# Attention and a two-layer MLP in one kernel: pools that wait tile by tile, a reordered end of attention, and the x of the next visit one unit earlier

## The chip, the cores and the metric

The kernel runs on one core of a Trainium2 chip. It drives five engines: PE (TensorE, matrix products), DVE (VectorE), ACT (ScalarE), POOL (GpSimd) and SP (SyncE, which here only issues DMAs). The metric is the device time in microseconds (us) of one launch, as a median of several runs.

## The reference

q, k and v are 8 x 8 heads of 576 positions by 64. Attention is causal with a decay that comes from f, and its result, rearranged to 4608 tokens by 512, is x of a two-layer MLP with 2048 features. All is float32.

```python
def _attn_ref(q, k, v, f):
    scores = scale * np.matmul(q, k.transpose(0, 1, 3, 2))
    cum = np.cumsum(np.log(np.clip(f, 0.0001, 1.0)), axis=-1)
    decay = cum[:, :, :, None] - cum[:, :, None, :]
    scores = np.where(causal, -1000000000.0, scores + decay)
    ...
    return np.matmul(attn, v)

def _moe_ref(x, w_in, w_out):
    h = x @ w_in
    sp = np.maximum(h, 0.0) + np.log1p(np.exp(-np.abs(h)))
    g = h * erf(sp)
    return g @ w_out
```

## The kernel before

**Attention** walks through 64 steps, one step for each half of the rows of a pair of heads, as a software pipeline in the loop of line 615: step t computes scores of t (PE), then the reduction and exponentials (DVE, ACT), normalizes t-2 (POOL), transposes the probabilities of t-3 (`transposes`, PE, into three rotating PSUM banks t), empties these banks into pt (`evacuate`, ACT and DVE), multiplies with v for t-4 (`values`, PE, into o) and writes the finished o of t-5 to xo and, for each pair of heads, to the DRAM buffer xt_d (`store`). xt_d is x transposed. The last of these stores is issued by ACT's queue, all others by SP's. Beside all this the weights are converted from words to sums and to high and low halves in DRAM (wi_d, wo_d).

**The MLP** works on 9 visits. A visit is 768 tokens with a run of feature units of 256 features: visits 0 to 2 have 5 units each (units 0 to 14), visits 3 to 5 have 3 units (15 to 23), visits 6 to 8 have 8 units (24 to 47). Both products are done in two float32r halves, high and low (high x high, high x low, low x high). The up product (`up`, line 164) goes by Strassen-like 2x2 blocks: 7 products (n = 0 to 6) into four PSUM banks pha, phb, phx and phy. `up(u, 0)` computes products 0 to 3 (a, b, x, y) and `up(u, 1)` products 4 to 6 (a, x, y). Each product n needs its own x, `xs{k}_n` for visit k: a quarter of x as loaded (r11, r12, r22, r21, by `load_x`), or a difference of quarters (T1, T2, 12, T4, by `sub`: on POOL for visits up to 3, on DVE later). ACT casts it to its high half (`high`, line 135) and POOL subtracts for its low half (`low`, line 140). The subtraction "12" overwrites r12 and uses r22, T4 uses r21 and T2. The raw quarters and differences share 6 buffers, the xs 10 in pool xp and 3 in pool xq.

The loop of line 683 does one unit after another. In the slot of unit u PE computes y of unit u (`down`, 36 matmuls) and then the up products of unit u+2. `middle` (line 279) also makes the activations of unit u+1 on ACT, multiplies them with h on DVE (`gate`), casts to gh on ACT and subtracts to gl on POOL (`round_gate`); it empties the y banks on DVE (`flush`), and calls `combine` and `prepare`, which make the x of the next visit: `SPLITS` says which n are prepared in which unit of the current visit. Because up runs two units ahead, the first up of visit k+1 runs in the last unit but one of visit k.

**What sets the order.** On PE, ACT, DVE and POOL instructions run in the order of the code (line 308). SP's DMAs are put in order by the framework. A pool that is opened over the memory of closed pools waits, by default, for everything that used those old pools: ep and ps_h (line 669) follow the pools io and ps_s, wop, xq, yp and ps_y (line 673) follow wk, ps_t and ps_o of attention. wop holds wo, the second layer's weights of a unit, in two buffers; wp holds wi, the first layer's, in two. `load_wi(u + 4)` comes at the end of a unit, and a wi buffer is free again when the up that read it is done.

In the profile the names of tiles are given without numbers: xs, r and rT are x of a product, a loaded quarter, a difference; t, pt, o and xo belong to attention; e is an activation, u a sum of up banks.

Of the kernel before, what the change touches and what calls it, by code (L numbers as in the profile page):

```python
# [73 lines left out]
class Moe:  # L74
# [13 lines left out]
    PRODUCTS = [("P1", "a"), ("P6", "b"), ("P7", "x"), ("P5", "y"), ("P2", "a"), ("P4", "x"), ("P3", "y")]  # L88
    FIRST = 4
    X = ["11", "T2", "12", "T1", "21", "T4", "22"]  # L90
    SPLITS = {3: [[0, 3, 4, 6], [1, 2, 5]], 5: [[0, 4], [3, 6], [1, 2], [5]], 8: [[0], [4], [3], [6], [1], [2], [5]]}
    TILES = ["11", "21", "22", "12"]

    def __init__(self, tc, xt_d, out, xp, wp):
# [35 lines left out]
                out=raw[k, name][:, kd], in0=raw[k, a][:, kd], in1=raw[k, b][:, kd], op=ALU.subtract)  # L130

    def high(self, k, n):
        pool, bufs = (self.xq, 3) if k % 2 and n in (3, 4, 6) else (self.xp, 10)
        self.xs[k, n] = x = pool.tile([P, 2, 2, TB], F32R, name=f"xs{k}_{n}", tag="xs", bufs=bufs)
        self.nc.scalar.copy(out=x[:, 0], in_=self.raw[k, self.X[n]])

# [109 lines left out]
    def flush(self, u, tb, y):  # L246
# [8 lines left out]
        if a == feats[-1]:  # L255
            row = v * NW + tb * P
            nc.sync.dma_start(out=self.out[row:row + P] if a == NU - 1 else self.part_d[v * NTB + tb], in_=ys)

    def combine(self, u, between):

        k, i, a = self.units[u]
        if k + 1 < len(self.visits):
            four = [4 in n for n in self.SPLITS[len(self.visits[k][1])]].index(True) + 1
            names = ("T2", "12") if between else ("T1",)
            for name in names if i == 0 else ("T4",) if i == four and not between else ():
                self.sub(k + 1, name)

    def prepare(self, u):

        k, i, a = self.units[u]  # L270
        splits = self.SPLITS[len(self.visits[k][1])]
        if k + 1 < len(self.visits) and i < len(splits):
            for n in splits[i]:
                self.high(k + 1, n)
                self.low(k + 1, n)
            if i == len(splits) - 1:
                self.load_x(k + 2)

    def middle(self, u, convert):

# [23 lines left out]
def attention_moe(ctx, tc, q2, k2, vp, f, w_in, w_out, out):  # L304
# [134 lines left out]
    def convert(steps):  # L439
        for call, *args in steps:  # L440
            call(*args)

    moe_pools = ctx.enter_context(ExitStack())
    with ExitStack() as ph:
# [167 lines left out]
        load_weight(1)  # L612
        work = schedule(range(NU1 + 1))[:8 * NU1 + 5]
        work[-1] = [step for step in work[-1] if step[0] is in_low]
        for t in range(NH + 5):
            there = [0 <= t - n < NH for n in range(6)]
            p, half = divmod(t, 2)
            if half == 0 and t + 4 < NH:
                load(p + 2)
            if half == 0 and there[2]:  # L620
                load_values(p - 1)
            if t == X0:
                moe.load_x(0)
                moe.later = moe.x_steps(0)
            if t == NH - 6:
                moe.load_wi(0)
                moe.load_wi(1)
            if NH <= t < NH + 4:
                moe.up((t - NH) // 2, (t - NH) % 2)
                if t == NH + 1:  # L630
                    moe.load_wi(2)
            if there[2]:
                normalize(t - 2)
            if there[5]:
                store(t - 5)
            if there[0]:
                scores(t)
            if there[1]:
                exps(t - 1, 0)
            if there[0]:  # L640
                reduce(t, 0)
            if there[3]:
                for a in range(3):
                    transposes(t - 3, a)
                evacuate(t - 3, 0)
            if there[3] and len(BANKS[(t - 3) % 2]) == 4:
                transposes(t - 3, 3)
            if there[4]:
                values(t - 4)
            if there[1]:  # L650
                exps(t - 1, 1)
            if there[0]:
                reduce(t, 1)
            if there[3]:
                for a in range(1, len(BANKS[(t - 3) % 2])):
                    evacuate(t - 3, a)
            due = 2 * t + 2 if t < 4 else 8 + (8 * NU1 - 4) * (t - 3) // (NH - 4)
            while work and 8 * NU1 + 5 - len(work) < due:
                convert(work.pop(0))
            if t > X0 and moe.later:  # L660
                convert([moe.later.pop(0)])
            if t == NH + 1:
                moe.activate(0)
                for n in range(4):
                    moe.gate(0, n)
                    moe.round_gate(0, n)
            if t == NH - 1:
                early.close()
                moe.ep = moe_pools.enter_context(tc.tile_pool(name="ep", bufs=2, side="right"))
                moe.ps_h = moe_pools.enter_context(tc.tile_pool(name="ps_h", bufs=1, space=PSUM, side="right"))  # L670
        assert not work and not moe.later and not pts and not held and not vals

    moe.wop = ctx.enter_context(tc.tile_pool(name="wop", bufs=1))
    moe.xq = ctx.enter_context(tc.tile_pool(name="xq", bufs=1))
    moe.yp = ctx.enter_context(tc.tile_pool(name="yp", bufs=1))
    moe.ps_y = ctx.enter_context(tc.tile_pool(name="ps_y", bufs=1, space=PSUM))
    moe.load_wo(0)
    moe.load_wo(1)
    moe.load_wi(3)
    moe.load_x(1)  # L680
    moe.want_y(0)
    work = beside_units()
    for u in range(moe.n):
# [42 lines left out]
```

## Time and profile before

| | us |
|---|---|
| median of 3 timed runs | 1153.01 |
| their range | 1152.77 to 1154.39 |
| the profiled execution, as a run | 1155.79 |
| its span, first to last instruction | 1154.0 |
| busy: PE / DVE / ACT / POOL | 1097.6 / 839.1 / 711.5 / 634.9 |
| DMA, moved bytes | 280.11 MB |
| mean granted clock of PE | 0.982 |

How to read it: a row of the timeline gives the start, the busy time of the group, the engine, the line, the operation, and out<-in by the program's names; x32 is the number of instructions, and brackets give the idle time before them and what ended it. A row of the waits gives the waiting engine and line, what it waited for, the sum in us, how often, and the longest. Attention fills the first 380 us, the units the rest; the first y matmul starts at 390.35 and unit 16 at 643.97. Line numbers here are those of the kernel before; below line 259 the changed kernel's lines are 7 higher, and more from the attention loop on.

### The profile page before, as it was taken

To read this page: it belongs to the slowest core of one execution; us is meant where nothing else is said; L and a number is where in the kernel's file an instruction comes from. 1 tells how busy PE (TensorE), PEld (TensorE's weight loads), DVE (VectorE), ACT (ScalarE), POOL (GpSimd) and SP (SyncE) were. 2 spreads that over 40 slices of the span, in tenths; PEclk is the share of its full clock that TensorE was granted. 3 is DMA by queue.
4 is the path that set the end of the run, shared out by engine and by line. 5 is a ranking of instruction groups with operands and counts; after the bars stand their busy time and mean duration, and the time that the engine had idled before them with its cause. 6 is when DMAs were issued, how large, how long until landed. Compare 5 with 4: busy or idle time off the path is not lost.

```text
span 1154.0 us, 21827 instructions
## 1 busy us (share of the span) xinstructions
PE 1097.6 (95%) x7552; PEld 964.3 (84%) x7552; DVE 839.1 (73%) x1940; ACT 711.5 (62%) x1540; POOL 634.9 (55%) x758
## 2 busy tenths in 40 slices
PE   5999899999998599999999898989999999999998
PEld 3788788788888588988889787879888999988897
DVE  7898878989994399899766666667666666666655
ACT  3687867788785356565665554645565555555553
POOL 1676657877785197696863827363433344433223
PEclk9999999999999899999999998989999999999999
DMA  8698898888864468869688675856555755575432
GB/s 296 212 334 281 312 371 268 294 272 279 275 251 160 164 248 291 321 246 377 217 308 289 213 273 192 289 167 247 214 205 201 255 175 174 191 247 192 182 137 91
DMA packets 75725, 280.11 MB, mean 243 GB/s; under 512 B 7904, under 2 KB 17120, under 8 KB 63328
## 3 DMA queue, kind: packets, MB, share of 16 engines
q1 hardware_dynamic: 75472, 278.43, 68.2%
q8 instruction: 60, 0.98, 0.3%
q14 instruction: 49, 0.40, 0.1%
q10 hardware_dynamic: 144, 0.29, 0.1%
HBM read 231.88 MB, written 46.81 MB: 242 GB/s over the span
## 4 chain that ended last, share of the span: by engine, by line
PE 55%; DVE 4%; POOL 1%; issue 1%; ACT 0%; POOLq 0%; DVEq 0%; ACTq 0%
PE y L233 28%; PE phy L175 8%; PE phx L175 8%; PE pha L175 7%; PE phb L175 4%; DVE rT L129 1%; DVE ys L254 1%; DVE e L214 1%; DVE r L129 1%; POOL gl L222 0%; POOL xs L140 0%; DVE u L181 0%; ACT gh L221 0%; ACT L206 0%; ACT e L206 0%
## 5 line engine op out<-in xcount | busy, mean ns | idle before, releaser
L222 POOL TENSOR_TENSOR gl<-e,gh 128x384 fp32r<-128x384 f32 x192 | 219.6, 1175 | 379.6 <-PE y L233 323.1
L233 PE MATMUL y<-wo,gh 128*128 128x512 f32 x1152 | 358.2, 392 | 12.7 <-issue 10.7
L233 PEld LDWEIGHTS y<-wo,gh 128*128 128x128 f32 x1152 | 216.1, 189 | 58.4 <-issue 10.8
L537 POOL TENSOR_SCALAR pr<-pr,st 128x576 f32<-128x576 f32 (+4 forms) x320 | 164.1, 534 | 123.8 <-DVE st L533 80.0
L233 PE MATMUL y<-wo,gl 128*128 128x512 f32 x576 | 225.8, 392 | 0.0
L254 DVE TENSOR_TENSOR ys<-y,ys 128x512 f32<-128x512 f32 x252 | 172.5, 688 | 69.6 <-PE y L233 69.6
L526 ACT ACTIVATE pr<-pr,st 128x576 f32<-128x576 f32 (+3 forms) x320 | 176.7, 556 | 4.0 <-DVE st L514 4.0
L514 DVE CUSTOM_DVE_ANT_0 pr<-s,c 128x576 f32<-128x576 f32 (+3 forms) x320 | 136.4, 486 | 27.8 <-PE s L496 17.1
L221 ACT CAST gh<-e 128x384 fp32r<-128x384 f32 x192 | 94.1, 513 | 73.7 <-DVE e L214 72.4
L204 ACT ACTIVATE e<-pha 128x384 f32<-128x384 f32 x48 | 23.6, 492 | 185.0 <-PE pha L175 176.3
L491 PE MATMUL s<-k,q 64*128 64x320 f32 (+4 forms) x768 | 121.6, 429 | 14.7 <-DMA k<-in_k_dram 8.3
L233 PEld LDWEIGHTS y<-wo,gl 128*128 128x128 f32 x576 | 108.7, 189 | 22.9
L175 PE MATMUL pha<-xs,wi 128*128 128x384 f32 x576 | 118.7, 341 | 4.2 <-DVE e L214 4.1
L204 ACT ACTIVATE e<-u 128x384 f32<-128x384 f32 x144 | 74.8, 522 | 73.2 <-DVE u L181 70.4
L491 PEld LDWEIGHTS s<-k,q 64*128 64x128 f32 x768 | 81.2, 197 | 46.0 <-issue 18.8
L175 PE MATMUL phx<-xs,wi 128*128 128x384 f32 x576 | 118.7, 341 | 0.6 <-POOL xs L140 0.6
L558 ACT COPY pt<-t 128x512 f32<-128x512 f32 x128 | 73.6, 577 | 72.3 <-PE t L549 68.3
L175 PE MATMUL phy<-xs,wi 128*128 128x384 f32 x576 | 118.0, 340 | 0.0
L175 PEld LDWEIGHTS pha<-xs,wi 128*128 128x128 f32 x576 | 104.1, 191 | 8.5 <-DVE e L214 4.2
L576 PE MATMUL o<-pt,v 128*64 128x128 f32 (+1 forms) x1920 | 103.8, 261 | 7.5 <-DMA v<-in_vp_dram 3.2
L576 PEld LDWEIGHTS o<-pt,v 128*64 128x64 f32 x1920 | 95.1, 138 | 17.3 <-issue 5.4
L181 DVE TENSOR_TENSOR u<-phx,u 128x384 f32<-128x384 f32 x96 | 53.4, 556 | 76.8 <-PE phx L175 76.1
(68 smaller groups left out, 1723.8 us busy)
## 6 DMA issues: line engine op xcount, KB each, us to landing
wi<-wi_d SPq DMA_DIRECT2D x48, 1792.0 KB, 7.5
wo<-wo_d SPq DMA_DIRECT2D x48, 1024.0 KB, 4.9
v<-in_vp_dram SPq DMA_DIRECT2D x32, 576.0 KB, 7.4
c<-cum_d SPq DMA_DIRECT2D x62, 288.0 KB, 6.0
r<-xt_d SPq DMA_DIRECT2D x36, 384.0 KB, 5.2
q<-in_q_dram SPq DMA_DIRECT2D x32, 320.0 KB, 5.7
k<-in_k_dram SPq DMA_DIRECT2D x32, 288.0 KB, 5.9
out_dram<-ys SPq DMA_DIRECT2D x36, 256.0 KB, 4.8
```

Of the source, the lines that this page charges most:

```text
L175: nc.tensor.matmul(out=ps, lhsT=wi[:, w, n, kd], rhs=xs[:, x, kd], start=not part and kd == 0 and i == 0, stop=kd == 1 and i == 2, skip_gr ...
L204: nc.scalar.activation(out=e_, in_=h[c], func=AF.Softplus)
L221: nc.scalar.copy(out=gh, in_=e_)
L222: nc.gpsimd.tensor_tensor(out=gl, in0=e_, in1=gh.bitcast(F32), op=ALU.subtract)
L233: nc.tensor.matmul(out=y, lhsT=x[:, cs], rhs=wo[:, i, w], start=i == 0 and n == 0, stop=i == 1 and n == 2)
L254: nc.vector.tensor_tensor(out=ys, in0=y, in1=ys, op=ALU.add)
L491: nc.tensor.matmul(out=s[j][:, at:at + k1 - k0], lhsT=q[h, PAD + START[i]:PAD + END[i]], rhs=k[h, k0:k1], start=i > 0, stop=k1 < END[i])
L514: nc.vector.tensor_tensor_reduce(out=to[:, ::-1] if j else to, in0=score, in1=decay_, scale=-0.125, scalar=BIG, op0=ALU.add, op1=ALU.min, ...
L526: nc.scalar.activation(out=seg, in_=seg, func=AF.Exp, bias=st[:, 0, j, m:m + 1], scale=-1.0, accum_out=st[:, 1, j, m:m + 1])
L537: nc.gpsimd.tensor_scalar(out=seg, in0=seg, scalar1=st[:, 2, j, m:m + 1], scalar2=1.0, op0=ALU.mult, op1=ALU.mult)
L558: nc.scalar.copy(out=pt[:, 512 * a:512 * a + 512], in_=b)
L576: nc.tensor.matmul(out=o[h, to:to + width], lhsT=v[:, ch, h], rhs=pt[:, at[j]:at[j] + width], start=n == 0, stop=n == len(parts) - 1, skip ...
```

## The change

Three things are changed.

- The pools ep, ps_h, wop, xq, yp and ps_y are opened with `reuse_waits="tile"`: a tile of them waits only for those tiles of the old pools whose memory it takes.
- The end of attention is reordered. `up(1, 0)` comes after the last transpositions and values, `up(0, ..)` after `normalize`, the stores of steps 61 to 63 come one step sooner, and the loop is one step shorter. The quarters of x of visit 1 are loaded in attention's step 63, and its differences T1, T2 and 12 and its product 0 are made at the end of attention.
- `ahead(u)` gives the place that `combine` and `prepare` work on: one unit further than before, and in the last unit of a visit the first place for the visit after next. So the x of a visit is made one unit sooner. Product 6 leaves `SPLITS` and is made at the start of the last unit but one (`combine`), with the next load of quarters behind it; xq now holds products 3, 4 and 5 of odd visits.

```diff
--- before.py
+++ after.py
@@ -88,7 +88,7 @@
     PRODUCTS = [("P1", "a"), ("P6", "b"), ("P7", "x"), ("P5", "y"), ("P2", "a"), ("P4", "x"), ("P3", "y")]
     FIRST = 4
     X = ["11", "T2", "12", "T1", "21", "T4", "22"]
-    SPLITS = {3: [[0, 3, 4, 6], [1, 2, 5]], 5: [[0, 4], [3, 6], [1, 2], [5]], 8: [[0], [4], [3], [6], [1], [2], [5]]}
+    SPLITS = {3: [[0, 3, 4], [1, 2, 5]], 5: [[0], [3, 4], [1, 2], [5]], 8: [[0], [3], [4], [1], [2], [5]]}
     TILES = ["11", "21", "22", "12"]
 
     def __init__(self, tc, xt_d, out, xp, wp):
@@ -130,7 +130,7 @@
                 out=raw[k, name][:, kd], in0=raw[k, a][:, kd], in1=raw[k, b][:, kd], op=ALU.subtract)
 
     def high(self, k, n):
-        pool, bufs = (self.xq, 3) if k % 2 and n in (3, 4, 6) else (self.xp, 10)
+        pool, bufs = (self.xq, 3) if k % 2 and n in (3, 4, 5) else (self.xp, 10)
         self.xs[k, n] = x = pool.tile([P, 2, 2, TB], F32R, name=f"xs{k}_{n}", tag="xs", bufs=bufs)
         self.nc.scalar.copy(out=x[:, 0], in_=self.raw[k, self.X[n]])
 
@@ -256,25 +256,32 @@
             row = v * NW + tb * P
             nc.sync.dma_start(out=self.out[row:row + P] if a == NU - 1 else self.part_d[v * NTB + tb], in_=ys)
 
+    def ahead(self, u):
+
+        k, i, a = self.units[u]
+        return (k + 2, 0) if i == len(self.visits[k][1]) - 1 else (k + 1, i + 1)
+
     def combine(self, u, between):
 
-        k, i, a = self.units[u]
-        if k + 1 < len(self.visits):
-            four = [4 in n for n in self.SPLITS[len(self.visits[k][1])]].index(True) + 1
-            names = ("T2", "12") if between else ("T1",)
-            for name in names if i == 0 else ("T4",) if i == four and not between else ():
-                self.sub(k + 1, name)
+        k, i = self.ahead(u)
+        if k >= len(self.visits):
+            return
+        if i < 2:
+            for name in ("T2", "12") if between and i == 0 else () if between else ("T1", "T4")[i:i + 1]:
+                self.sub(k, name)
+        if i == len(self.visits[k - 1][1]) - 1 and not between:
+            self.high(k, 6)
+            self.low(k, 6)
+            self.load_x(k + 1)
 
     def prepare(self, u):
 
-        k, i, a = self.units[u]
-        splits = self.SPLITS[len(self.visits[k][1])]
-        if k + 1 < len(self.visits) and i < len(splits):
-            for n in splits[i]:
-                self.high(k + 1, n)
-                self.low(k + 1, n)
-            if i == len(splits) - 1:
-                self.load_x(k + 2)
+        k, i = self.ahead(u)
+        if k < len(self.visits):
+            for n in self.SPLITS[len(self.visits[k - 1][1])][i:i + 1]:
+                for m in n:
+                    self.high(k, m)
+                    self.low(k, m)
 
     def middle(self, u, convert):
 
@@ -612,7 +619,13 @@
         load_weight(1)
         work = schedule(range(NU1 + 1))[:8 * NU1 + 5]
         work[-1] = [step for step in work[-1] if step[0] is in_low]
-        for t in range(NH + 5):
+
+        def units(t):
+            moe.up((t - NH) // 2, (t - NH) % 2)
+            if t == NH + 1:
+                moe.load_wi(2)
+
+        for t in range(NH + 4):
             there = [0 <= t - n < NH for n in range(6)]
             p, half = divmod(t, 2)
             if half == 0 and t + 4 < NH:
@@ -625,14 +638,12 @@
             if t == NH - 6:
                 moe.load_wi(0)
                 moe.load_wi(1)
-            if NH <= t < NH + 4:
-                moe.up((t - NH) // 2, (t - NH) % 2)
-                if t == NH + 1:
-                    moe.load_wi(2)
             if there[2]:
                 normalize(t - 2)
-            if there[5]:
+            if there[5] and t < NH + 2:
                 store(t - 5)
+            if t in (NH, NH + 1, NH + 3):
+                units(t)
             if there[0]:
                 scores(t)
             if there[1]:
@@ -659,25 +670,36 @@
                 convert(work.pop(0))
             if t > X0 and moe.later:
                 convert([moe.later.pop(0)])
+            if t > NH and there[4]:
+                store(t - 4)
             if t == NH + 1:
                 moe.activate(0)
                 for n in range(4):
                     moe.gate(0, n)
                     moe.round_gate(0, n)
             if t == NH - 1:
+                moe.load_x(1)
+            if t == NH + 2:
+                units(t)
+                moe.sub(1, "T1")
+                moe.sub(1, "T2")
+            if t == NH + 3:
+                moe.sub(1, "12")
+                moe.high(1, 0)
+                moe.low(1, 0)
+            if t == NH - 1:
                 early.close()
-                moe.ep = moe_pools.enter_context(tc.tile_pool(name="ep", bufs=2, side="right"))
-                moe.ps_h = moe_pools.enter_context(tc.tile_pool(name="ps_h", bufs=1, space=PSUM, side="right"))
+                moe.ep = moe_pools.enter_context(tc.tile_pool(name="ep", bufs=2, side="right", reuse_waits="tile"))
+                moe.ps_h = moe_pools.enter_context(tc.tile_pool(name="ps_h", bufs=1, space=PSUM, side="right", reuse_waits="tile"))
         assert not work and not moe.later and not pts and not held and not vals
 
-    moe.wop = ctx.enter_context(tc.tile_pool(name="wop", bufs=1))
-    moe.xq = ctx.enter_context(tc.tile_pool(name="xq", bufs=1))
-    moe.yp = ctx.enter_context(tc.tile_pool(name="yp", bufs=1))
-    moe.ps_y = ctx.enter_context(tc.tile_pool(name="ps_y", bufs=1, space=PSUM))
+    moe.wop = ctx.enter_context(tc.tile_pool(name="wop", bufs=1, reuse_waits="tile"))
+    moe.xq = ctx.enter_context(tc.tile_pool(name="xq", bufs=1, reuse_waits="tile"))
+    moe.yp = ctx.enter_context(tc.tile_pool(name="yp", bufs=1, reuse_waits="tile"))
+    moe.ps_y = ctx.enter_context(tc.tile_pool(name="ps_y", bufs=1, space=PSUM, reuse_waits="tile"))
     moe.load_wo(0)
     moe.load_wo(1)
     moe.load_wi(3)
-    moe.load_x(1)
     moe.want_y(0)
     work = beside_units()
     for u in range(moe.n):
```

**The passage from attention to the units.** PE in the kernel before, from values of step 61 on (o61): up of unit 1 (pha1 to phy1) stands ahead of the transpositions t63.

```order
L576 MATMUL o61_5342<-pt61_5253,v30_5035 64x128 x10
L576 MATMUL o61_5342<-pt61_5253,v30_5035 64x64 x6
L175 MATMUL pha1_5397<-xs0_0_3257,wi1_4727 128x384 x6
L175 MATMUL phb1_5404<-xs0_1_3502,wi1_4727 128x384 x6
L175 MATMUL phx1_5411<-xs0_2_3740,wi1_4727 128x384 x6
L175 MATMUL phy1_5418<-xs0_3_3992,wi1_4727 128x384 x6
L549 MATMUL t63_0_5436<-ident_63,pr63_5141 128x128 x4
L549 MATMUL t63_1_5441<-ident_63,pr63_5141 128x128 x4
L549 MATMUL t63_2_5446<-ident_63,pr63_5141 128x128 x4
L549 MATMUL t63_3_5452<-ident_63,pr63_5141 128x128
L576 MATMUL o62_5454<-pt62_5325,v31_5204 64x128 x10
L576 MATMUL o62_5454<-pt62_5325,v31_5204 64x64 x4
```

PE at the same place in the changed kernel:

```order
L583 MATMUL o61_5350<-pt61_5261,v30_5035 64x128 x10
L583 MATMUL o61_5350<-pt61_5261,v30_5035 64x64 x6
L556 MATMUL t63_0_5409<-ident_63,pr63_5141 128x128 x4
L556 MATMUL t63_1_5414<-ident_63,pr63_5141 128x128 x4
L556 MATMUL t63_2_5419<-ident_63,pr63_5141 128x128 x4
L556 MATMUL t63_3_5425<-ident_63,pr63_5141 128x128
L583 MATMUL o62_5427<-pt62_5333,v31_5212 64x128 x10
L583 MATMUL o62_5427<-pt62_5333,v31_5212 64x64 x4
L175 MATMUL pha1_5447<-xs0_0_3257,wi1_4727 128x384 x6
L175 MATMUL phb1_5454<-xs0_1_3502,wi1_4727 128x384 x6
L175 MATMUL phx1_5461<-xs0_2_3740,wi1_4727 128x384 x6
L175 MATMUL phy1_5468<-xs0_3_3992,wi1_4727 128x384 x6
```

The seven rows of up(1, ..) now stand together behind the transpositions t63 and the values o62. Behind them, in both kernels, come o63 and the first y.

DVE at this place in the kernel before, from the emptying of bank t62_2: the gates of unit 0 (e0), the sums of up(1, 0), the store of step 61 (L588, L589), and the emptying of t63_2 (L556).

```order
L556 COPY pt62_5325<-t62_2_5336 128x512
L214 TENSOR_TENSOR e0_11_5364<-e0_11_5364,pha0_5206 128x384
L214 TENSOR_TENSOR e0_21_5368<-e0_21_5368,u1_0_5240 128x384
L214 TENSOR_TENSOR e0_22_5366<-e0_22_5366,u3_0_5235 128x384
L214 TENSOR_TENSOR e0_12_5370<-e0_12_5370,u2_0_5234 128x384
L185 COPY u2_1_5425<-pha1_5397 128x384
L181 TENSOR_TENSOR u2_1_5425<-phb1_5404,u2_1_5425 128x384
L181 TENSOR_TENSOR u3_1_5426<-phx1_5411,u2_1_5425 128x384
L181 TENSOR_TENSOR u3_1_5426<-phy1_5418,u3_1_5426 128x384
L588 COPY xo30_5323<-o61_5342 128x256
L589 COPY xo30_5323<-o61_5342 128x64
L556 COPY pt63_5435<-t63_2_5446 128x512
```

DVE in the changed kernel, from the last sum of up(0, 1) on:

```order
L181 TENSOR_TENSOR u2_0_5251<-phy0_5244,u2_0_5251 128x384
L563 COPY pt62_5333<-t62_2_5344 128x512
L595 COPY xo30_5309<-o61_5350 128x256
L596 COPY xo30_5309<-o61_5350 128x64
L214 TENSOR_TENSOR e0_11_5375<-e0_11_5375,pha0_5223 128x384
L214 TENSOR_TENSOR e0_21_5379<-e0_21_5379,u1_0_5257 128x384
L214 TENSOR_TENSOR e0_22_5377<-e0_22_5377,u3_0_5252 128x384
L214 TENSOR_TENSOR e0_12_5381<-e0_12_5381,u2_0_5251 128x384
L563 COPY pt63_5408<-t63_2_5419 128x512
L561 COPY pt63_5408<-t63_3_5425 128x64
L592 COPY xo31_5445<-o62_5427 128x2x128
```

The store of step 61 has moved ahead of the gates, and the emptying of t63_2 (now L563) stands directly behind them, ahead of the sums of unit 1. In the built program the transposition t63_3 takes the bank of t63_2 and waits for L563 (before, it took that of t63_0, which ACT empties).

SP's DMAs at this place, before (wi_d4 and wo_d5 are parts of converted weights, xt_d the store of heads 60 and 61) and with the change:

```order
L387 DMA wo_d5_115<-wtop20_4802 128x512
L592 DMA xt_d_83<-xo30_5323 128x576
L155 DMA wi3_5533<-wi_d3_105 128x3584
L161 DMA wo0_5529<-wo_d0_110 128x2048
L161 DMA wo1_5531<-wo_d1_111 128x2048
```

```order
L155 DMA wi2_5331<-wi_d2_104 128x3584
L599 DMA xt_d_83<-xo30_5309 128x576
L155 DMA wi3_5553<-wi_d3_105 128x3584
L161 DMA wo0_5549<-wo_d0_110 128x2048
L161 DMA wo1_5551<-wo_d1_111 128x2048
```

The first two wo follow wi of unit 3 in both. The store of a converted weight (L387) that stood ahead of the store of xt_d is no longer there: it now comes behind the two wo.

**A visit's end.** POOL in the kernel before, from the last gl of unit 16 on (gl16_12; gl of unit 16 is made in the slot of unit 15), up to the products of visit 4:

```order
L222 TENSOR_TENSOR gl16_12_8067<-e16_12_8037,gh16_12_8066 128x384
L140 TENSOR_TENSOR xs4_0_8070<-r11_4_7761,xs4_0_8070 128x384 x2
L140 TENSOR_TENSOR xs4_3_8074<-rT1_4_8028,xs4_3_8074 128x384 x2
L140 TENSOR_TENSOR xs4_4_8078<-r21_4_7767,xs4_4_8078 128x384 x2
L140 TENSOR_TENSOR xs4_6_8082<-r22_4_7765,xs4_6_8082 128x384 x2
L222 TENSOR_TENSOR gl17_11_8219<-e17_11_8195,gh17_11_8218 128x384
L222 TENSOR_TENSOR gl17_21_8223<-e17_21_8199,gh17_21_8222 128x384
L222 TENSOR_TENSOR gl17_22_8227<-e17_22_8197,gh17_22_8226 128x384
L222 TENSOR_TENSOR gl17_12_8231<-e17_12_8201,gh17_12_8230 128x384
L140 TENSOR_TENSOR xs4_1_8234<-rT2_4_8123,xs4_1_8234 128x384 x2
L140 TENSOR_TENSOR xs4_2_8238<-r12_4_7763,xs4_2_8238 128x384 x2
L140 TENSOR_TENSOR xs4_5_8242<-rT4_4_8192,xs4_5_8242 128x384 x2
```

POOL in the changed kernel, from the last gl of unit 15 on:

```order
L222 TENSOR_TENSOR gl15_12_7915<-e15_12_7879,gh15_12_7914 128x384
L140 TENSOR_TENSOR xs4_0_7918<-r11_4_7722,xs4_0_7918 128x384 x2
L140 TENSOR_TENSOR xs4_3_7922<-rT1_4_7870,xs4_3_7922 128x384 x2
L140 TENSOR_TENSOR xs4_4_7926<-r21_4_7728,xs4_4_7926 128x384 x2
L222 TENSOR_TENSOR gl16_11_8075<-e16_11_8051,gh16_11_8074 128x384
L222 TENSOR_TENSOR gl16_21_8079<-e16_21_8055,gh16_21_8078 128x384
L222 TENSOR_TENSOR gl16_22_8083<-e16_22_8053,gh16_22_8082 128x384
L222 TENSOR_TENSOR gl16_12_8087<-e16_12_8057,gh16_12_8086 128x384
L140 TENSOR_TENSOR xs4_1_8090<-rT2_4_7979,xs4_1_8090 128x384 x2
L140 TENSOR_TENSOR xs4_2_8094<-r12_4_7724,xs4_2_8094 128x384 x2
L140 TENSOR_TENSOR xs4_5_8098<-rT4_4_8048,xs4_5_8098 128x384 x2
L140 TENSOR_TENSOR xs4_6_8203<-r22_4_7726,xs4_6_8203 128x384 x2
```

The products 0, 3 and 4 of visit 4 now stand behind gl of unit 15 instead of unit 16, the products 1, 2 and 5 behind gl of unit 16 instead of unit 17, and product 6 behind those.

## The prediction

> **What bounds the kernel now.** I read the page first, then the table of PE's waits from the end of attention on, then windows cut at the first matmul of a unit, then the timeline around the waits.
>
> ```profile
> span 1154.0 us, 21827 instructions
> PE 1097.6 (95%) x7552; PEld 964.3 (84%) x7552; DVE 839.1 (73%) x1940; ACT 711.5 (62%) x1540; POOL 634.9 (55%) x758
> PE 55%; DVE 4%; POOL 1%; issue 1%; ACT 0%; POOLq 0%; DVEq 0%; ACTq 0%
> ```
>
> PE is busy for 95% of the span and leads the chain that ended last. No matmul is removed, so only two things can come back: PE's idle time, 1154.0 − 1097.6 = 56.4 us, and time lost at a lower clock, which counts as busy. From 340 us on, PE's waits are:
>
> ```profile
> PE y L233 <- issue: 10.7, 1, 10.7
> PE phb L175 <- ACT xs L135: 6.4, 3, 2.2
> PE phb L175 <- POOL xs L140: 5.9, 3, 2.0
> PE pha L175 <- DVE e L214: 4.1, 1, 4.1
> PE y L233 <- DVE ys L254: 2.0, 4, 0.5
> PE phx L175 <- POOL xs L140: 0.6, 1, 0.6
> ```
>
> Nearly all of it lies at five places: the passage from attention to the units (10.7 and 4.1), three waits for x of a next visit (phb), and one small one of that kind (phx). The windows give their whole price, with what the clock adds:
>
> ```profile
> 612.99:628.47 15.48, 15.48 (x80) 14.03 (x79) 9.36 (x16) 8.22 (x15) 4.61 (x4) 1.00 0.93 317
> 643.97:667.68 23.71, 19.14 (x79) 16.34 (x79) 14.13 (x22) 10.53 (x18) 14.54 (x14) 0.86 0.54 189
> 698.70:722.37 23.67, 19.11 (x80) 16.31 (x80) 14.13 (x22) 10.53 (x18) 14.52 (x14) 0.86 0.54 189
> 753.38:777.02 23.64, 19.05 (x80) 16.26 (x79) 14.14 (x22) 10.53 (x18) 14.54 (x14) 0.86 0.55 190
> 439.21:456.21 17.00, 16.34 (x80) 13.90 (x80) 15.94 (x23) 10.53 (x18) 13.62 (x11) 1.00 0.69 242
> ```
>
> Columns: length, busy time of PE, weight loads, DVE, ACT, POOL, then the clock, the DMA share and GB/s. The first row is an undisturbed unit, 15.5 us with PE always busy. The next three (units 16, 19 and 22, the middle ones of the three-unit visits) take 8.2, 8.2 and 8.1 us more: 4.6 us idle, and 3.6 us of matmuls at a clock of 0.86. The last (unit 3) takes 1.5 more.
>
> **x one unit sooner at three-unit visits.** What PE waits for in unit 16:
>
> ```profile
> 653.48 4.20 POOL L222 TENSOR_TENSOR gl<-e,gh 128x384 fp32r<-128x384 f32 x4 [4.94 <-PE y L233]
> 655.41 0.83 ACT L135 CAST xs<-rT 128x768 fp32r<-128x768 f32 x1
> 656.29 0.44 PE L175 MATMUL phb<-xs,wi 128*128 128x384 f32 x1 [2.13 <-ACT xs L135]
> 657.65 1.94 POOL L140 TENSOR_TENSOR xs<-rT,xs 128x384 fp32r<-128x384 f32 x2
> 658.68 1.97 PE L175 MATMUL phb<-xs,wi 128*128 128x384 f32 x5 [1.96 <-POOL xs L140]
> 660.45 2.12 PE L175 MATMUL phx<-xs,wi 128*128 128x384 f32 x6
> ```
>
> Unit 18 is the first of the next visit. The high half of its second product's x (the cast, L135) is made in the very unit that multiplies with it, behind the gates' casts, and the low half (L140) behind POOL's four gl. PE stands twice, then runs phb, phx and phy cold (2.12 us for what takes 1.20 warm). After the change x of products 1, 2 and 5 is made one unit sooner: the low half that lets phb go on at 658.68 would be there 15.5 us earlier, near 643, ten us before phb wants it. That of product 6 is made at the start of the unit whose last group (phy) reads it. Both waits and the cold matmuls go: 8.20 + 8.16 + 8.13 = **24.5 us**, against the 15.51 of a unit.
>
> What is late next? DVE's subtractions and the y banks they hold up:
>
> ```profile
> 629.13 1.02 DVE L129 TENSOR_TENSOR rT<-r,r 128x384 f32<-128x384 f32 x2
> 641.52 2.60 DVE L129 TENSOR_TENSOR rT<-r,rT 128x384 f32<-128x384 f32 x2
> 643.66 4.89 POOL L140 TENSOR_TENSOR xs<-r,xs 128x384 fp32r<-128x384 f32 x4
> 644.04 2.66 DVE L129 TENSOR_TENSOR r<-r,r 128x384 f32<-128x384 f32 x2
> 647.75 1.69 DVE L129 TENSOR_TENSOR rT<-r,rT 128x384 f32<-128x384 f32 x2
> 650.09 0.73 PE L233 MATMUL y<-wo,gh 128*128 128x512 f32 x2 [0.48 <-DVE ys L254]
> ```
>
> A pair of subtractions takes 1.02 us alone and 2.60 to 2.66 beside POOL's low halves, and DVE then empties y late: 0.48 us of wait, about 0.8 of the 8.2. After the change the same three pairs stand at the end of one unit and the start of the next, but with six low halves on POOL instead of eight; these end about 2.4 us sooner (half of the 4.89 for four), at 646.1, so the third pair should take 1.02 and the wait should vanish. I take nothing for it; its bounds are 0 and +0.8 at each of three visits. The gl of such a unit end at 653.48 + 4.20 = 657.68, 13.7 us into it, and are wanted at 15.5: 1.8 us of cover. ACT's cast of product 6 ahead of the activations takes 0.83 us of that engine, which waits for PE's products there (ACT is busy 10.5 of 23.7 us).
>
> [...]
>
> **x one unit sooner at the five-unit visits.** Unit 3's phx waits for product 5's low half; that is made one unit sooner, so its **1.5 us** go. The same edit moves POOL's and DVE's work in the first 13 units, beside the conversion of weights. There one unit already waits for DVE's late emptying of y (2.0 us in four waits, of which three are the 0.48 to 0.5 of the three-unit visits). This may go or return at the two other boundaries among these units: 0, with bounds of −0.5 and +1.0. Eight-unit visits lose nothing now and gain nothing.
>
> **The passage from attention to the units.** SP's waits and ACT's store first, then PE and DVE:
>
> ```profile
> SPq L161 <- DMA xt_d<-xo: 5.0, 1, 5.0
> ```
>
> ```profile
> 358.85 0.69 DVE L556 COPY pt<-t 128x512 f32<-128x512 f32 x1 [0.15 <-PE t L549]
> 364.47 1.49 DVE L214 TENSOR_TENSOR e<-e,u 128x384 f32<-128x384 f32 x3
> 364.61 2.29 PE L175 MATMUL pha<-xs,wi 128*128 128x384 f32 x6 [4.10 <-DVE e L214]
> 370.41 1.67 PE L549 MATMUL t<-ident,pr 128*128 128x128 f32 x13
> 375.69 1.20 PE L175 MATMUL phy<-xs,wi 128*128 128x384 f32 x6
> 372.23 1.97 POOL L129 TENSOR_TENSOR rT<-r,r 128x384 f32<-128x384 f32 x2
> 376.92 0.32 SPq L155 DMA_DIRECT2D wi<-wi_d  x1
> 380.25 0.35 ACTq L592 DMA_DIRECT2D xt_d<-xo  x1
> 385.39 0.80 SPq L161 DMA_DIRECT2D wo<-wo_d  x2
> 390.35 1.19 PE L233 MATMUL y<-wo,gh 128*128 128x512 f32 x2 [10.72 <-issue]
> ```
>
> ```profile
> wo<-wo_d SPq DMA_DIRECT2D x1, 1024.0 KB, 4.7
> wo<-wo_d SPq DMA_DIRECT2D x2, 1024.0 KB, 5.8
> wi<-wi_d SPq DMA_DIRECT2D x1, 1792.0 KB, 7.6
> ```
>
> PE's 10.7 us "issue" is a wait for the first wo, which may be loaded only when everything in attention's old pools is done. The last of that is the store of the last heads, issued 380.25 and landed 5.0 later; SP issues wo at 385.39, it lands 4.7 later, at 390.1, and y starts at 390.35. With waits for single tiles the first wo no longer needs that store. In SP's program it stands right behind the load of wi for unit 3, which waits for the end of the second up product. So I need that end, then one queue.
>
> The end: in the new order PE's last transposition needs a bank that DVE empties behind the four gates. The gates end at 364.47 + 1.49 = 365.96, that copy takes 0.69 (row 358.85 is one of the same line), so PE resumes near 366.6 instead of 364.61, with twelve transpositions (about 1.5 us of the 1.67 for 13) already done. The rest is the same work, from 364.61 to 376.89 before: 366.6 + 12.3 − 1.5 ≈ 377.4. The wait thus stays, and wi goes out 0.5 us later. Its bytes land 7.6 us after issue, at 385.0. For the queue: the two wo were issued 0.4 us apart; the second took 2 × 5.8 − 4.7 = 6.9, so it landed 2.6 behind the first. One wo behind wi then lands at 385.0 + 2.6 = 387.6, and y starts at 387.8: **2.5 us** sooner. Bounds: if wi and both wo came together, 390.4 (nothing); if the first wo needed only its own 4.7, 377.4 + 4.7 + 0.2 = 382.3 (8.0 us). I take the middle, since the nearest row is the pair of wo, whose landings follow each other. PE is idle for over 7 us either way, so the first y stay cold (1.19 us for two at 390.35, 0.73 at 650.09) and win nothing.
>
> [...]
>
> Three more subtractions and one x are made in attention's tail, on POOL (1.97 us a pair, row 372.23) and ACT (0.83), while PE waits for wo: nothing.
>
> **The sum.** 24.5 + 1.5 + 2.5 = 28.5 us. The profiled execution took 1155.79 (its span 1154.0), so it would be 1127.3; the timed median, 1153.01, is 2.8 below that execution, and from it I get **1124.5**.
>
> **The rivals.**
> - **B: wo overtakes wi.** [...] Against: both come off one queue, and wi alone takes 7.6. It gives 8.0 instead of 2.5: 1119.0.
> - **C: a smaller wait remains at the boundaries.** The third pair of subtractions again meets POOL (2.6 instead of 1.02), y is emptied later, gl comes past its 1.8 us of cover. For it: the slow rows 641.52 and 644.04. Against: two low halves fewer. At 0.8 to 3 us for each of three visits: 1127 to 1133.5.
> - **D: x is ready no sooner.** The loads r of a visit also feed it; if they came late, the three waits would stay at 8.2 and only 4.0 us be won: 1149. Did the tile waits not bite either, it would be within 0.2%, about what a measurement can tell from no change. Against: what these loads wait for, POOL's low halves of the visit before, is done a unit sooner as well.
> - **E: slower, by SP's order.** The next visit's r loads stand on SP ahead of a wi and wait until POOL has used up a half of x. If POOL's lows for products 5 and 6, now in another unit, held r long, wi would come after PE's need and every boundary would stall. A wi is issued when the up before it ends (376.89 and 376.92 above), and its own up begins at least one unit of 15.5 us later; it takes 7.6, which leaves 7.9 us of cover. Slower than before needs r to block SP for 7.9 + 28.5/8 = 11.5 us at each of the eight boundaries. At 13 us it gives 8 × 5.1 − 28.5 = +12.3: 1165. Against: POOL is busy 14.5 of the 23.7 us of such a unit and 4.6 of the 15.5 of the one before it, so its lows cannot stand for 13 us.
>
> **How the numbers follow.** Forecast 0.61, B 0.10, C 0.20, D 0.06, E 0.03. The range must leave out no more than 2 in 10: below it holds B with the early units' bound and what y may still win (1119.0 − 1.5 = 1117.5), above C's top with the passage's worst (1133.5 + 2.5 = 1136.0). Faster: forecast, B, C and most of D, 0.95; same 0.02; slower 0.03.
>
> **What would show it.** Windows of units 16, 19 and 22 at 15.5 to 16.3 us with a clock of 1.00; no phb row among PE's waits; unit 3 at 15.5. PE's wait "issue" before the first y at 7 to 9 us instead of 10.7, with wo issued within 1 us of wi near 377.5 and landing about 2.6 behind it. The wait behind the gates stays near 4 us but moves to a transposition. It is wrong if those three units stay above 17 us, if new waits at y or pha show up in the first 13 units, or if the wo lands before wi.

## The result and the profile after

The changed kernel takes **1123.28 us** (median of 4 runs, 1122.45 to 1127.5) against 1152.89 for the kernel before (4 runs); the ratio is 0.9752, with an interval of 0.9723 to 0.9782. The forecast was 1124.5, with a range of 1117.5 to 1136. The profiled execution took 1127.5, 28.3 less than that of before.

The page of the changed kernel, its span and its engines:

```profile
span 1125.7 us, 21838 instructions
PE 1086.0 (96%) x7552; PEld 957.9 (85%) x7552; DVE 835.3 (74%) x1940; ACT 711.1 (63%) x1540; POOL 633.5 (56%) x758
```

PE's waits from 340 us on, in the same columns as before. The rows shown before have become two; nothing waits for x any more.

```profile
PE y L233 <- DMA wo<-wo_d: 8.9, 1, 8.9
PE t L556 <- DVE pt L563: 4.8, 1, 4.8
```

The windows of the changed kernel for units 16, 19, 22 and 3 (the four that were long), of unit 0, and of units 6 and 7. Columns as before: length, busy time of PE, weight loads, DVE, ACT and POOL, clock, DMA share, GB/s.

```profile
639.99:655.50 15.51, 15.51 (x80) 14.07 (x79) 10.52 (x16) 8.34 (x15) 10.56 (x11) 1.00 0.72 272
686.64:702.15 15.51, 15.51 (x79) 14.07 (x79) 10.52 (x16) 8.35 (x15) 10.54 (x11) 1.00 0.72 272
733.26:748.77 15.51, 15.51 (x79) 14.06 (x79) 10.52 (x16) 8.35 (x15) 10.45 (x11) 1.00 0.65 239
438.01:453.51 15.50, 15.50 (x79) 14.05 (x79) 14.08 (x21) 9.61 (x16) 13.70 (x12) 1.00 0.80 302
389.86:406.99 17.13, 17.13 (x78) 15.27 (x79) 11.24 (x17) 4.96 (x9) 9.60 (x9) 0.91 0.37 129
484.67:500.17 15.50, 15.50 (x79) 14.05 (x79) 14.60 (x22) 10.67 (x17) 12.39 (x13) 1.00 0.80 299
500.17:515.83 15.66, 15.66 (x80) 13.99 (x80) 15.06 (x22) 11.08 (x18) 11.68 (x10) 1.00 0.70 264
```

And of the kernel before, units 0, 6, 7 and 11, which were not shown:

```profile
390.35:408.19 17.84, 17.84 (x78) 15.78 (x79) 11.19 (x17) 4.96 (x9) 9.65 (x9) 0.86 0.31 111
487.22:502.93 15.71, 15.71 (x79) 13.98 (x79) 15.19 (x22) 10.77 (x17) 15.63 (x15) 1.00 0.67 241
502.93:519.27 16.34, 15.82 (x79) 13.98 (x79) 15.71 (x22) 11.09 (x18) 14.37 (x13) 1.00 0.63 236
565.79:581.94 16.15, 16.05 (x80) 13.97 (x79) 12.89 (x16) 10.45 (x18) 14.81 (x15) 1.00 0.62 224
```

The three middle units of the three-unit visits now look like any other: PE always busy, clock 1.00. From the first y to the end of the span it was 1154.0 − 390.35 = 763.65 us before and is 1125.7 − 389.86 = 735.84 now, 27.8 less. The passage, timeline rows of the kernel before (two that were not shown) and then of the changed one:

```profile
358.02 1.07 ACT L558 COPY pt<-t 128x512 f32<-128x512 f32 x2 [3.75 <-issue]
...
364.00 0.55 DVE L214 TENSOR_TENSOR e<-e,pha 128x384 f32<-128x384 f32 x1 [4.45 <-ACT e L206]
```

```profile
359.25 1.07 ACT L565 COPY pt<-t 128x512 f32<-128x512 f32 x2 [3.75 <-issue]
...
365.23 0.56 DVE L214 TENSOR_TENSOR e<-e,pha 128x384 f32<-128x384 f32 x1 [2.99 <-ACT e L206]
...
367.93 0.45 PE L556 MATMUL t<-ident,pr 128*128 128x128 f32 x1 [4.84 <-DVE pt L563]
368.31 2.83 PE L583 MATMUL o<-pt,v 128*64 128x128 f32 x28
...
378.12 1.21 PE L175 MATMUL phy<-xs,wi 128*128 128x384 f32 x6
...
379.36 0.32 SPq L155 DMA_DIRECT2D wi<-wi_d  x1
...
389.86 1.22 PE L233 MATMUL y<-wo,gh 128*128 128x512 f32 x2 [8.95 <-DMA wo<-wo_d]
```

The two executions are not alike in attention itself: the same ACT copy and the first gate come 1.23 us later in the second one. Counted from the first gate, the first y came after 26.35 us before and comes after 24.63 now, 1.7 sooner. The landings of the changed kernel's wi and first wo there, in us from their issue, say what the 8.95 us are spent on: wi is there at 387.0, wo 2.8 later.

```profile
wi<-wi_d SPq DMA_DIRECT2D x1, 1792.0 KB, 7.6
wo<-wo_d SPq DMA_DIRECT2D x1, 1024.0 KB, 10.1
```

### The profile page after: what moved, and what is told of

It is laid out like the page before. It is cut to its first block, busy times and chain, and to the rows that moved or that the text cites. A ratio compares the mean times of both kernels' runs of the same rounds, so it can differ in the third digit from the quotient of the medians.

```text
span 1125.7 us, 21838 instructions
## 1 busy us (share of the span) xinstructions
PE 1086.0 (96%) x7552; PEld 957.9 (85%) x7552; DVE 835.3 (74%) x1940; ACT 711.1 (63%) x1540; POOL 633.5 (56%) x758
## 4 chain that ended last, share of the span: by engine, by line
PE 89%; DVE 4%; DMA 4%; ACT 1%; issue 1%; POOL 0%; SPq 0%; POOLq 0%; DVEq 0%; ACTq 0%
PE y L233 35%; PE pha L175 9%; PE phx L175 9%; PE phy L175 9%; PE s L498 8%; PE o L583 7%; PE t L556 6%; PE phb L175 4%; DMA v<-in_vp_dram 3%; PE s L503 2%; DVE pr L521 1%; DMA wo<-wo_d 1%; DVE pt L563 0%; DMA fd<-in_f_dram 0%; DVE wtop L366 0%
## 5 line engine op out<-in xcount | busy, mean ns | idle before, releaser
L175 PE MATMUL phx<-xs,wi 128*128 128x384 f32 x576 | 115.3, 334 | 0.0
L175 PE MATMUL phy<-xs,wi 128*128 128x384 f32 x576 | 115.3, 334 | 0.0
L556 PE MATMUL t<-ident,pr 128*128 128x128 f32 x800 | 105.6, 279 | 5.1 <-DVE pt L563 4.8
```

Source lines behind the costliest of these rows:

```text
L175: nc.tensor.matmul(out=ps, lhsT=wi[:, w, n, kd], rhs=xs[:, x, kd], start=not part and kd == 0 and i == 0, stop=kd == 1 and i == 2, skip_gr ...
L556: nc.tensor.transpose(out=b[:, n * P:(n + 1) * P], in_=probs[t][:, at:at + P], identity=ident)
```

## The experiments

Times are medians, each beside runs of the kernel before on the same chip (1149.9 to 1151.0 there, against 1152.9 above), so the ratios count. The sets differ: beside 1152.89 the change won 29.6 us, beside the 1150.38 of the second set 26.7 (experiment 4).

**1. The pools alone.** The kernel before, with the tile waits and nothing else:

```diff
-                moe.ep = moe_pools.enter_context(tc.tile_pool(name="ep", bufs=2, side="right"))
+                moe.ep = moe_pools.enter_context(tc.tile_pool(name="ep", bufs=2, side="right", reuse_waits="tile"))
...
-    moe.wop = ctx.enter_context(tc.tile_pool(name="wop", bufs=1))
+    moe.wop = ctx.enter_context(tc.tile_pool(name="wop", bufs=1, reuse_waits="tile"))
```

> The kernel before, with reuse_waits="tile" on the six pools and nothing else. Theory (the first wo stands in SP's queue behind wi of unit 3, and they land one after the other): wi goes out at 376.9 as before, wo0 right behind it, and lands about 10 us later, near 387, so the first y starts 3 to 3.5 us sooner than 390.35; 1149 to 1150.5 us. Rival (wo0 needs only its own 4.7 us): first y near 382, 1144 to 1145. Rival (the pools gain nothing by themselves, all of the passage's gain is by the new order): 1152.5 to 1153.5. The three long units (16, 19, 22) stay at 23.7 us.

1146.57 against 1150.98, ratio 0.9970 (0.9953 to 0.9988). Two rows of its timeline:

```profile
371.24 0.32 SPq L155 DMA_DIRECT2D wi<-wi_d  x1
...
381.89 1.22 PE L233 MATMUL y<-wo,gh 128*128 128x512 f32 x2 [7.95 <-DMA wo<-wo_d]
```

And the landings of its wi and first wo:

```profile
wi<-wi_d SPq DMA_DIRECT2D x1, 1792.0 KB, 7.5
wo<-wo_d SPq DMA_DIRECT2D x1, 1024.0 KB, 10.2
```

From wi's issue to the first y it is 10.65 us, against 390.35 − 376.92 = 13.43 before: 2.8 us sooner. The wo issued 0.4 us behind wi lands 10.2 us after its own issue, 3.1 behind wi, where it took 4.7 alone. wi itself lands 7.5 us after its issue, as it did before with no wo behind it (7.6). So behind wi it is the wo that lands later, by 5.5 us, and not wi. By the clock time alone the first y, 381.89, looks like the rival with 4.7 us (382), and 1146.57 us lies between what the two expected; but attention ended sooner in this execution (last section), and counted from wi's issue the rivals (4.7 us, or nothing) fall. The gain of the time, 4.4 by the medians, has an interval of 1.4 to 5.4.

**2. x one unit sooner, alone.** The kernel before with `ahead`, the new `high`, `combine`, `prepare` and `SPLITS`, and for the first unit:

```diff
     moe.want_y(0)
+    for name in ("T1", "T2", "12"):
+        moe.sub(1, name)
+    moe.high(1, 0)
+    moe.low(1, 0)
```

> The kernel before, with only x of a visit made one unit sooner (ahead, SPLITS, combine, prepare, xq); the differences T1, T2, 12 and product 0 of visit 1 are made just ahead of the first unit. Theory (the one unit is what removes the waits): units 16, 19 and 22 go from 23.7 to 15.5-15.7 us, unit 3 from 17.0 to 15.5, units 5, 6 and 11 lose what they were over; 24.2 + 1.5 + 1.4 = 27 us, so 1125 to 1127. Rival (the tile waits are needed for x to come sooner, since xq stood behind the old pools): 1135 to 1150. The wait of PE before the first y stays at 10 to 11 us.

1126.63, ratio 0.9788 (0.9758 to 0.9817): 24.4 us by itself. The two longest of the three waits that PE has left from 340 us on (the third is 1.1 at o):

```profile
PE y L233 <- DMA wo<-wo_d: 11.3, 1, 11.3
PE pha L175 <- DVE e L214: 4.1, 1, 4.1
```

And the window of unit 16:

```profile
639.45:654.96 15.51, 15.51 (x80) 14.07 (x80) 10.53 (x16) 8.35 (x15) 10.53 (x11) 1.00 0.73 272
```

The phb and phx waits are gone without the tile waits, so x does not need them. Units 3, 6, 7 and 11 (the expectation numbers two of them one too low) are at 15.5 as well. The time lies in the range expected only because the kernel before is 2 us faster on this chip: 27 us were expected to go and 24.4 went (interval 21 to 28). In this profile the units do give 27.1, but from the first gate to the first y it takes 28.08 us instead of 26.35, with slower matmuls in up(1, 0) (1.11 us for the last three of phx, 0.68 before), and unit 0 lasts 18.27 instead of 17.84. Why was not tried.

**3. Product 6 alone.** Is it the unit in which the products are made, or less work beside the waits? Here only product 6 moves, to the start of the second unit of a three-unit visit:

```diff
-    SPLITS = {3: [[0, 3, 4, 6], [1, 2, 5]], 5: [[0, 4], [3, 6], [1, 2], [5]], 8: [[0], [4], [3], [6], [1], [2], [5]]}
+    SPLITS = {3: [[0, 3, 4], [1, 2, 5]], 5: [[0, 4], [3, 6], [1, 2], [5]], 8: [[0], [4], [3], [6], [1], [2], [5]]}
...
+            if i == 1 and not between and len(self.visits[k][1]) == 3:
+                self.high(k + 1, 6)
+                self.low(k + 1, 6)
```

> The kernel before, with one thing of the change: at visits of three units product 6 leaves SPLITS and is made at the start of the second unit; products 1, 2 and 5 stay where they were. Theory (what counts is that products 1, 2, 5 are made in the very unit that reads them): ACT's cast of product 1 still comes behind the gates' casts, so PE's phb waits stay near 2 + 2 us and units 16, 19, 22 stay at 22 to 23.7 us; 1149 to 1153. Rival (the cause is the load on POOL and DVE of that unit and the one before, which two low halves fewer relieve): phb waits shrink under 1 us, the three units fall to 16 to 19 us, 1130 to 1140.

1151.08 against 1150.98, ratio 1.0004 (0.9985 to 1.0024). Its waits, then its unit 16, then unit 16 of experiment 1, where x is made as before:

```profile
PE phb L175 <- ACT xs L135: 6.3, 3, 2.1
PE phb L175 <- POOL xs L140: 5.6, 3, 2.0
```

```profile
638.40:660.77 22.37, 17.82 (x80) 14.99 (x80) 14.13 (x22) 10.53 (x18) 14.56 (x14) 0.92 0.56 200
```

```profile
634.69:657.03 22.34, 17.79 (x80) 14.97 (x80) 14.13 (x22) 10.53 (x18) 14.55 (x14) 0.92 0.57 200
```

The waits stay, so moving product 6 by itself wins nothing. But the rival is not tried by this run: POOL is busy for 14.56 us in this unit (14.54 in the kernel before) and DVE for 14.13 (the same), because product 6's low halves still stand behind those of product 4 in POOL's order. And the rival is not empty, as a row of ACT in this unit shows:

```profile
641.70 1.19 ACT L204 ACTIVATE e<-u 128x384 f32<-128x384 f32 x2 [4.22 <-DVE u L181]
```

ACT stands for 4.2 us until DVE has made the sums that come behind its slow subtractions (in the kernel before these take 2.60 and 2.66 us, ahead of a wait of 4.21), and its cast for product 1 comes later by that. Experiment 2 moves both, the products and these subtractions, one unit ahead: it shows that the edit removes the waits, not which of the two moves does. No run moves the subtractions alone. The two windows above are alike, so the 22.4 instead of 23.7 us is not from product 6: the idle time is the same in all three executions (4.57 us before, 4.55 in both rows), and only the clock of the unit differs (0.92 against 0.86).

**4. Without the new order of attention's end.** Experiments 1 and 2 together.

> The two other parts together, without the reordered end of attention: tile waits and x one unit sooner, attention's last steps in the order of before. Theory (the new order of attention's end buys nothing, since it puts PE's last transposition behind the gates): the parts add up, 3.5 + 27 us, so 1121.5 to 1123.5, no slower than the whole change (1123.3). Rival (the reorder is what lets the parts work together, and is worth 2 us or more): 1125.5 or above.

1123.99, ratio 0.9770 (0.9742 to 0.9798), beside 0.9752 and, in a second set, 0.9766 (0.9744 to 0.9789; 1123.69 us) for the whole change; 1121.5 to 1123.5 was expected. Within the intervals the parts add up, and the new order gains nothing that can be measured in the time. Its waits show what it exchanges: the 4.1 at pha and 1.1 at o, in place of 4.8 at the last transposition.

```profile
PE pha L175 <- DVE e L214: 4.1, 1, 4.1
PE o L583 <- DVE xo L592: 1.1, 1, 1.1
```

The second set was run for the two waits that the change leaves, with the changed kernel again:

> The changed kernel itself, beside the next three on one chip. Its time 1121 to 1125 us; PE's wait at the last transposition near 4.8 us and before the first y near 9 us, as in its first profile.

It took 1123.69 us, with the same two waits of 8.9 and 4.8 us.

**5. The first wo ahead of wi on SP.** In the changed kernel (`load_wi` and `load_wo` return their DMA for it):

```diff
-    moe.load_wo(0)
-    moe.load_wo(1)
-    moe.load_wi(3)
+    first = moe.load_wo(0), moe.load_wo(1)
+    wi3 = moe.load_wi(3)
+    for wo in first:
+        tc.add_manual_dep(wi3.ins, wo.ins.name, mybir.DependencyInfo(
+            mybir.DependencyClass.NoSync, mybir.DependencyReason.DATA), reason="wo ahead of wi on SP")
```

> The changed kernel with the loads of wo for units 0 and 1 put ahead of wi of unit 3 on SP (an order edge, no other change). Theory (wo0 needs nothing but its place in the queue: its memory is that of a tile of step 62 which PE has read by 360): it goes out right behind the store at 362 and lands near 370; PE's wait of 8.9 us before the first y goes to under 1 us, the first y are no longer cold (8.4 instead of 10.0 us for unit 0); 9 + 1.6, so 1112 to 1114 us. Rival (the landing is limited by something else, such as the transfers around it, or another wait takes its place: the activations of unit 1 or the emptying of y): the first y starts at 384 or later, or unit 0's slot is longer than 17.1 us; 1117 to 1123.

1113.88 against 1123.69, ratio to before 0.9682 (0.9655 to 0.9709). SP issues the first wo at 360.23, behind the store. The one row of PE's waits from 340 us on:

```profile
PE t L556 <- DVE pt L563: 4.8, 1, 4.8
```

The landing of the first wo:

```profile
wo<-wo_d SPq DMA_DIRECT2D x1, 1024.0 KB, 9.2
```

The timeline of PE at the first y:

```profile
376.69 1.66 PE L583 MATMUL o<-pt,v 128*64 128x128 f32 x32
378.28 0.72 PE L233 MATMUL y<-wo,gh 128*128 128x512 f32 x2
```

Behind wi of unit 2 and a store it takes 9.2 us here too, but nobody waits. The first y follows o at once and runs as fast as a y at a clock of 1.00 (0.72 us for two; 0.73 at 650.09 in the kernel before, at 1.00, and 1.22 in the changed kernel, at 0.50). The theory holds.

**6. The gates later.** In the changed kernel, unit 0's gates stand behind the emptying of the banks of step 63:

```diff
             if t == NH + 1:
                 moe.activate(0)
-                for n in range(4):
-                    moe.gate(0, n)
-                    moe.round_gate(0, n)
...
             if t == NH + 2:
+                for n in range(4):
+                    moe.gate(0, n)
+                    moe.round_gate(0, n)
                 units(t)
```

> The changed kernel with the gates of unit 0 put behind the emptying of the banks of step 63 on DVE (and ahead of up of unit 1), nothing else. Theory (PE's 4.8 us at the last transposition are DVE's order, the copy behind four gates that wait for ACT's erf): the wait shrinks to under 1.2 us there, a shorter one comes at pha of unit 1, which needs the first gate; up of unit 1 ends 5 to 6 us sooner, wi and the first wo go out as much sooner and the first y too; 1116.5 to 1119. Rival (the wait only moves: up of unit 1 starts no sooner, since pha's bank is read by the first gate, or PE then runs cold for as long): 1121 to 1124.

1118.36, ratio 0.9720 (0.9697 to 0.9743), 5.3 less than the changed kernel beside it. Its waits:

```profile
PE y L233 <- DMA wo<-wo_d: 9.2, 1, 9.2
PE pha L175 <- DVE e L214: 1.0, 1, 1.0
PE t L556 <- DVE pt L563: 0.9, 1, 0.9
```

The 4.8 us were DVE's order: 0.9 is left at the transposition, 1.0 at pha for the first gate. All behind it comes sooner, the wait for wo included, which stays as long.

**7. Both.** Experiments 5 and 6 together.

> Both edits. Theory: with wo there early, the first y follows PE's last attention matmul, and that one comes 5 to 6 us sooner by the later gates; PE hardly idles between attention and the units, so the gains add up, 10.5 + 5.5 and the rest of the cold clock: 1105 to 1108.5. Rival (y of unit 0 then waits for its own gh and gl, which the later gates delay, so the gains don't add): 1109 to 1114.

**1108.13 us**, ratio 0.9626 (0.9601 to 0.9652): 15.6 less than the changed kernel beside it, where the two alone gave 9.8 and 5.3. They add up, and this version beats both kernels. Its waits from 340 us on:

```profile
PE pha L175 <- DVE e L214: 1.0, 1, 1.0
PE t L556 <- DVE pt L563: 0.9, 1, 0.9
```

**8. The old end of attention with wo first.** Experiment 4 with the edit of 5, to see whether the new order pays once wo is there.

> Tile waits and x one unit sooner with attention's end in the order of before (as in e7_pools_x), and wo of units 0 and 1 ahead of wi of unit 3 on SP (as in e4_wo_first). Theory (the new order of attention's end buys nothing by itself, with or without the wait for wo): the first y follows the last attention matmul, about 8 us sooner than in e7_pools_x and warm, 10 to 10.5 us in all; 1112.5 to 1115, the same as e4_wo_first (1113.9). Rival (the new order is what lets wo be there early, because the store of step 61, which stands ahead of wo on SP, comes sooner with it): wo0 goes out only near 370 and PE waits for it, the first y at 381 or later; 1117 to 1122.

1112.60, ratio 0.9677 (0.9647 to 0.9707), against 0.9682 in experiment 5. The first y follows the last o here too; its wo, behind a store alone, is issued at 368.33 and is there when that y starts, at 375.80. So of the versions run the new order pays only with the later gates of experiment 6. Later gates in the old order were not run; there up of unit 1 itself waits for the first gate (the 4.1 us at pha).

## Why the prediction was right

- **x at three-unit visits** was the main term, 24.5 us. The three units went from 23.71, 23.67 and 23.64 to 15.51; units 15, 18 and 21 got 0.1 each, so 24.2 in these two executions. Experiment 2 shows that the edit does it alone. The prediction laid the waits to the place of the casts and low halves, which the rows bear out; that DVE's subtractions held ACT for 4.2 us ahead of them it left out, and the two were not separated. The size depends on the execution that it was read from: in experiment 3 the same three units lasted 22.37, 22.92 and 23.26, which is 22.0 over in place of 24.5: the idle part of the term is steady (4.31 to 4.55 us a unit there, 4.56 to 4.59 before), and the part from matmuls at a low clock differs between executions (PE busy for 2.3 to 3.2 us more than in a unit of 15.51 there, at clocks of 0.85 to 0.92; 3.5 to 3.6 before, at 0.86).
- **What is late next** was weighed rightly. Subtractions of visit 4 in the changed kernel:

```profile
621.93 2.60 DVE L129 TENSOR_TENSOR rT<-r,rT 128x384 f32<-128x384 f32 x2
624.45 2.66 DVE L129 TENSOR_TENSOR r<-r,r 128x384 f32<-128x384 f32 x2
628.16 1.02 DVE L129 TENSOR_TENSOR rT<-r,rT 128x384 f32<-128x384 f32 x2
```

  The two pairs beside POOL cost what they did, the third runs alone at 1.02, against 1.69 before (POOL's low halves end at 626.70), and the 0.5 us waits for ys are gone; the units 15, 18 and 21, in which the pairs now end, last 0.1 longer than others. Rival C priced a collision that the new order avoids for that pair.
- **Unit 3**: 17.00 to 15.50, the 1.5 forecast. **The early units** were mis-sized: I took 0, with bounds of −0.5 and +1.0. Units 6, 7 and 11 lasted 15.71, 16.34 and 16.15 and now 15.50, 15.66 and 15.50; unit 5 got 0.14, so 1.4 us were won, more than the upper bound. I had priced only the wait for ys, not the stretched matmuls of the other two. That of unit 11 is not in every execution of the old order (the unit lasted 16.14 in experiment 3, 15.51 in experiment 1).
- **The passage**: 2.5 forecast, and 1.7 + 0.7 = 2.4 measured, but by other parts. The queue term was right: 10.5 us from wi's issue (379.36) to the first y, 10.4 forecast. What PE does behind its restart was mis-sized: from the first gate to the end of up it takes 14.1 us, where 13.4 was forecast and 12.9 was the time before. PE resumes 2.7 us behind that gate, as forecast (2.6), but then values run at a low clock too (2.83 us for 1.54, at 0.50), and pha and phb give only part of that back (3.21 for 4.06). Unit 0 gave 0.7 back, which I had put at nothing: it lasts 17.13 instead of 17.84, at a clock of 0.91 instead of 0.86. It is 17.10 when the changed kernel is run again, and 17.68 to 18.27 in the five profiles with the old end of attention and the wait for wo; the length of the wait does not decide it (8.1 us and 18.05 in experiment 4). Why was not tried.
- **Rival B** fell by the rows above and experiment 1: behind wi the first wo lands 10.1 and 10.2 us after its issue, where it took 4.7 alone. **D** fell with the windows. **E**: in unit 16 the r loads and one of ys now stand ahead of wi, which goes out at 643.07, 3.1 us into the unit, instead of 0.2; that is within the 7.9 us of cover.

```profile
640.16 2.31 SPq L120 DMA_DIRECT2D r<-xt_d  x2
642.52 0.46 SPq L244 DMA_DIRECT2D ys<-part_d  x1
643.07 0.39 SPq L155 DMA_DIRECT2D wi<-wi_d  x1
```

The sum in the profiles is 24.2 + 1.5 + 1.4 + 2.4 = 29.5, less 1.2 for the later attention of that execution, which gives the 28.3 measured. The median of all runs is 29.6 lower (26.7 in the second set), and 28.5 was forecast. That the sum is so close is partly luck: the early units and unit 0 gave 2.1 us that were put at nothing, the first y came 0.8 less early than forecast, 0.3 was lost in units 15, 18 and 21, and the main term is 2.5 smaller in other executions of the old order.

## What to carry to other kernels

Where a wait is followed by slow matmuls, price the window of the whole unit, not the wait: here 4.3 to 4.6 us idle cost 6.9 to 8.2. When a wait for a pool goes, look at the queue behind which the released load then stands: the tile waits gave 2.8 us at the first wo, and one order edge that puts it ahead of a larger load gave 9.8 more. And when steps are reordered, follow each bank or buffer to the engine that frees it: the new order of attention's end paid only when DVE's copy no longer stood behind four gates.

## What was not expected of the hardware

Executions of the same attention differ by 6 to 8 us. A mark that all kernels here share is a group of 32 matmuls of values just ahead of the gates. It started at 358.84 in the kernel before, and in experiment 1, with the same order of attention, at:

```profile
353.13 1.66 PE L576 MATMUL o<-pt,v 128*64 128x128 f32 x32
```

In the new order it started at 359.98 in the changed kernel, and in experiment 7, whose edits come behind it, at 352.20. The old order (six profiles) has 352.9 to 358.8, the new one (five) 352.2 to 360.0. The wait of PE for the loads of v between 100 and 340 us explains a part. In the kernel before it is as below, in experiment 3, with its mark at 352.9, it is 1.8, and in experiment 7 it is 0.6:

```profile
PE o L576 <- DMA v<-in_vp_dram: 3.2, 1, 3.2
```

The clock behind the wait adds to it: in the kernel before it is 0.50 from the end of the wait, 143.44, to 149.38, and a group of values takes 2.83 us there instead of 1.54. From 100 to 150 us, before and in experiment 1 (columns as above):

```profile
100.00:150.00 50.00, 46.35 (x527) 38.31 (x527) 37.41 (x142) 35.60 (x110) 32.94 (x58) 0.93 0.84 293
```

```profile
100.00:150.00 50.00, 48.58 (x593) 40.88 (x590) 42.34 (x166) 40.02 (x124) 33.66 (x59) 1.00 0.88 314
```

PE got through 527 matmuls in one and 593 in the other. Why the loads of v come later in some executions was not tried. It bears on how to read single profiles: a part of the kernel is better measured from a mark just ahead of it than from the start of the span.
